# Batches 0 and 1 of a fused attention and ELU-FFN kernel: weights in blocks of 1024 columns, eight shared PSUM banks and a given order of TensorE's first groups; halves of M merged in every batch

## The chip, the cores and the metric

The kernel runs on one core of a Trainium2 chip. The core has a matrix engine (TensorE, PE in the profile, with its weight loads as PEld), a vector engine (VectorE, DVE), a scalar engine (ScalarE, ACT), GpSimd (POOL), a queue engine (SyncE, SP) that issues most DMAs, and 16 DMA engines. Each engine runs its own instructions in the order in which they were emitted and waits for others through semaphores. TensorE writes only to PSUM, eight banks of 128 rows by 512 float32 values. The metric is the device time of one execution in microseconds (us).

## The reference

There are 8 batches of 8 heads with 512 tokens and 32 states of width 64. Each token attends to the states and each state to the tokens; the joined result (544 rows a batch, 512 wide) goes through a feed-forward layer with an ELU.

```python
def _attn_ref(x, state):
    scores = scale * np.matmul(x, state.transpose(0, 1, 3, 2))
    ...
    xread = np.matmul(a, state)           # a = softmax(scores)
    scores2 = scale * np.matmul(state, x.transpose(0, 1, 3, 2))
    ...
    sread = np.matmul(a2, x)              # a2 = softmax(scores2)
    return np.concatenate([xread, sread], axis=2).astype(np.float32)

def _moe_ref(x, w_in, w_out):             # x: (4352, 512)
    h = x @ w_in                          # w_in: 512 x 2048, float64
    g = np.where(h > 0.0, h, alpha * (np.exp(np.minimum(h, 0.0)) - 1.0))
    return (g @ w_out).astype(np.float32) # w_out: 2048 x 512, float64
```

The weights come as float64, 8 MB each, so that every weight has to be turned into float32 on the chip.

## The kernel before

**A planner orders everything.** The kernel first lists all operations in program order (`Plan.add`, each with an estimated cost and the tiles it reads and writes), then `Plan.run` plays them through once: each engine takes, of its ready operations, TensorE the one with the lowest number and every other engine the one that is due first (`set_due` works the due times back from TensorE's own order). The result is one fixed order for each engine, emitted at the end (lines 1366 to 1371). All operations are therefore recorded by one line of the kernel, L413; the fills of line 1361 are the exception. PSUM banks are given out in program order to the operations that open them, from six free banks; banks 6 and 7 are kept for one accumulator of the later batches (line 505). In the first 40 us of the plan, TensorE's idle time is filled with matmuls of the identity into bank 7 (`fill`).

**Weights.** `weight_block` (line 1015) loads a block of 64-bit words (128 rows, 512 values) by DMA into one of six raw buffers; `convert` (line 988) makes float32 of it with two ScalarE and four VectorE operations (`tensor_scalar` twice, `scalar_tensor_tensor`, and an unsigned add). There are 32 blocks: 16 of w_in, two for each of the eight column blocks `hc` of 256, and 16 of w_out. The float32 columns of w_in are kept in DRAM (`w_in_mem`) and fetched again for each later batch (`fetch`, into one of three slots, `hc % 3`).

**One batch.** Token attention is folded into the first layer: M = states times w_in (`make_m`, one half of a 512-wide chunk at a time, 16 small matmuls in a 64-row by 32-column tiling of the array), and h = a times M. `scores` (line 600) makes the scores, `softmax` (line 666) both softmaxes (VectorE, ScalarE, and GpSimd for two products), `state_read` reads for the states. In batches 0 and 1, `ffn1_plain` forms h with 512-wide matmuls, four groups for each of four chunks; from batch 2 on, `ffn1_chunk` and `ffn2` use Strassen-Winograd forms (seven products for eight), the second layer in two levels. Their sums of operands run on VectorE and GpSimd.

**The order of the program.** `start()` (line 1041) does batches 0 and 1 up to the middle of the second layer: a step `w_step(hc)` for each column block (convert, `make_m` for both batches, copy), with the attention and `ffn1` between them, then w_out's conversion and the second layer. Then `ffn2(o, 1, x1)` ends batch 1, `batch(b)` does batches 2 to 7, and `states()` the state rows of all batches. Each `ffn2` (line 1154) makes the scores, softmax and first half of M of the next batch in passing: `make_m` 0 and 1 stand ahead of the steps of `second[7]` (lines 1197 and 1199), `make_m` 2 and 3 ahead of those of `second[5]` (lines 1213 and 1214), 4 to 7 in `batch` (lines 1266 to 1275). `ident_ready` (line 1030) clears the two kept banks with four identity matmuls each.

## Time and profile before

| | |
|---|---|
| median of 3 runs | 726.34 us (725.87 to 726.53) |
| the profiled execution's own time | 725.68 us |
| its span, first to last instruction | 723.9 us |
| PE, PEld busy | 712.2, 594.0 us (98, 82%) |
| DVE, ACT, POOL busy | 544.9, 292.4, 131.3 us (75, 40, 18%) |
| TensorE clock granted | full, in all 40 slices |
| fills (L1361) | 148 matmuls |

A busy share is a union of instructions' times; TensorE's instructions overlap in its pipeline, so that its 98% also covers fills and short waits. A timeline line gives start, length, engine, line, operation, tiles (out<-in), shape and count; in brackets stand the idle time before it and what ended it. A matmul of float32 appears as two MATMUL instructions.

### The profile page before, as it was taken

To read this page: it belongs to the slowest core of one execution; us is meant where nothing else is said; L and a number is where in the kernel's file an instruction comes from. 1 tells how busy PE (TensorE), PEld (TensorE's weight loads), DVE (VectorE), ACT (ScalarE), POOL (GpSimd) and SP (SyncE) were. 2 spreads that over 40 slices of the span, in tenths; PEclk is the share of its full clock that TensorE was granted. 3 is DMA by queue.
4 is the path that set the end of the run, shared out by engine and by line. 5 is a ranking of instruction groups with operands and counts; after the bars stand their busy time and mean duration, and the time that the engine had idled before them with its cause. 6 is when DMAs were issued, how large, how long until landed. Compare 5 with 4: busy or idle time off the path is not lost.

```text
span 723.9 us, 14101 instructions
## 1 busy us (share of the span) xinstructions
PE 712.2 (98%) x5588; PEld 594.0 (82%) x5588; DVE 544.9 (75%) x1030; ACT 292.4 (40%) x576; POOL 131.3 (18%) x158
## 2 busy tenths in 40 slices
PE   9999999999999999999999999999999999999998
PEld 8744468888988798878988898879887898899886
DVE  2999999999658984898678975898489866976230
ACT  3899983011056213732074315621273207410320
POOL 0210000033111251108020521125110803000000
PEclk9999999999999999999999999999999999999999
DMA  9859970022262334425172326343442423000500
GB/s 231 265 123 320 293 254 29 1 52 96 88 146 82 100 84 120 114 59 138 70 172 61 81 67 150 103 104 84 117 117 59 125 81 118 1 1 30 152 27 25
DMA packets 133250, 78.52 MB, mean 108 GB/s; under 512 B 114240, under 2 KB 114752, under 8 KB 133184
## 3 DMA queue, kind: packets, MB, share of 16 engines
q1 hardware_dynamic: 130744, 76.96, 38.2%
q10 hardware_dynamic: 2440, 0.66, 0.5%
q8 instruction: 44, 0.72, 0.4%
q14 instruction: 22, 0.18, 0.1%
HBM read 61.34 MB, written 13.11 MB: 103 GB/s over the span
## 4 chain that ended last, share of the span: by engine, by line
PE 61%; DVE 29%; issue 3%; ACT 3%; POOL 2%; DMA 1%; SPq 1%; DVEq 0%; POOLq 0%; ACTq 0%
PE ps L413 60%; DVE g L413 7%; DVE sec L413 4%; DVE s L413 4%; DVE small L413 3%; DVE t_w L413 1%; POOL soft L413 1%; DVE w_out L413 1%; DVE ps L413 1%; DVE soft L413 1%; DVE o L413 1%; ACT xe L413 1%; DVE xr L413 1%; DVE m L413 1%; PE ps L1361 1%
## 5 line engine op out<-in xcount | busy, mean ns | idle before, releaser
L413 PE MATMUL ps<-w_out,g 128*128 128x256 f32 (+1 forms) x960 | 174.3, 332 | 0.5
L413 PEld LDWEIGHTS ps<-w_out,g 128*128 128x128 f32 x960 | 150.5, 191 | 21.1 <-ACT o L413 4.2
L413 PE MATMUL ps<-aT,m 128*128 128x256 f32 (+1 forms) x568 | 148.4, 407 | 1.2 <-ACT read L413 0.7
L413 PEld LDWEIGHTS ps<-aT,m 128*128 128x128 f32 x568 | 105.7, 190 | 32.6 <-issue 16.6
L413 DVE TENSOR_TENSOR o<-o,ps 128x128 f32<-128x128 f32 (+2 forms) x214 | 59.9, 286 | 60.2 <-PE ps L413 58.5
L413 POOL TENSOR_TENSOR m<-m 128x256 f32<-128x256 f32 x72 | 57.0, 810 | 192.4 <-ACT m L413 191.0
L413 ACT ACTIVATE xe<-ps 128x512 f32<-128x512 f32 x104 | 60.6, 599 | 59.2 <-PE ps L413 43.2
L413 PE MATMUL ps<-sec 128*128 128x128 f32 x544 | 73.5, 278 | 3.5 <-DVE o L413 3.5
L413 PEld LDWEIGHTS ps<-sec 128*128 128x128 f32 x544 | 66.2, 192 | 9.2 <-DVE o L413 7.1
L413 PE MATMUL ps<-t_w,s 128*128 128x128 f32 (+1 forms) x448 | 68.8, 305 | 0.0
L413 DVE SCALAR_TENSOR_TENSOR g<-xe,ps 128x512 f32<-128x512 f32 x56 | 37.1, 682 | 40.3 <-ACT xe L413 36.1
L413 PEld LDWEIGHTS ps<-t_w,s 128*128 128x128 f32 x448 | 62.6, 191 | 4.8 <-ACT m L413 0.8
L413 POOL TENSOR_TENSOR soft<-soft,small 128x512 f32<-128x512 f32 x32 | 35.1, 1101 | 153.4 <-DVE small L413 152.9
L413 ACT COPY o<-ps 128x128 f32<-128x128 f32 (+2 forms) x55 | 21.8, 408 | 85.3 <-PE ps L413 82.2
L413 ACT COPY ps<-ps 128x512 f32<-128x512 f32 x24 | 13.7, 570 | 95.8 <-PE ps L413 95.8
L413 ACT COPY m<-ps 128x512 f32<-128x512 f32 (+1 forms) x56 | 26.8, 530 | 57.5 <-PE ps L413 57.5
L413 PE MATMUL ps<-aT,s 128*128 128x256 f32 x168 | 41.5, 382 | 0.0
L413 DVE TENSOR_SCALAR xe<-xe 128x512 f32<-128x512 f32 x48 | 20.4, 431 | 27.7 <-ACT xe L413 27.5
L413 POOL TENSOR_TENSOR s<-s 128x256 f32<-128x256 f32 x24 | 17.0, 727 | 133.7 <-ACT s L413 133.2
L413 PE MATMUL ps<-w_half,kT 64*32 64x256 f32 x1024 | 39.8, 385 | 0.7 <-DVE g L413 0.4
L413 DVE TENSOR_TENSOR ps<-sec,ps 128x512 f32<-128x512 f32 x48 | 32.6, 690 | 8.3 <-PE ps L413 4.9
L413 ACT COPY sec<-ps 128x512 f32<-128x512 f32 x48 | 28.0, 584 | 22.4 <-PE ps L413 22.2
(112 smaller groups left out, 1074.4 us busy)
## 6 DMA issues: line engine op xcount, KB each, us to landing
w_half<-w_in_mem SPq DMA_DIRECT2D x56, 512.0 KB
t_w<-in_moe_w_in_dram SPq DMA_DIRECT2D x16, 512.0 KB
t_w<-in_moe_w_out_dram SPq DMA_DIRECT2D x16, 512.0 KB
out_dram<-o SPq DMA_DIRECT2D x14, 512.0 KB
xe<-in_x_dram SPq DMA_DIRECT2D x26, 256.0 KB
o<-in_x_dram SPq DMA_DIRECT2D x80, 64.0 KB
w_in_mem<-w_half SPq DMA_DIRECT2D x8, 512.0 KB
xr<-xr SPq DMA_DIRECT2D x96, 32.0 KB
```

The source lines that it names most:

```text
L413: ins = getattr(engine, name)(**{k: resolve(v) for k, v in kw.items()})
L1361: nc.tensor.matmul(psum[:, 7, :P], ident, ident, start=False, stop=True, skip_group_check=True)
```

## The change

Seven things change. **Weights** come in blocks of 1024 values (three raw buffers, 16 blocks); only the first block of w_in is loaded and converted in two parts. **The first loads** have a given order (`FIRST_LOADS`), and the states of batch 0 and of batch 1 are turned apart. **The program's order** in `start()`: `ffn1` of batch 0, chunk 0, stands ahead of `turn_state` and of batch 1's attention, and `ffn1` of batch 1 ahead of `turn_state(1)`; `FIRST_PE` gives 70 of TensorE's operations in `start()` other places in its order (an operation's `turn`), among them the first products of the second layer, and `EARLIER` shifts the due times of some 70 operations. **PSUM**: all eight banks are shared until the kept ones are first used, and an operation takes a free bank whenever it can run, not in program order. `ident_ready` now depends on the last TensorE operation of `start()`; fills go to any bank that the plan has free, from 0.5 us of idle time on and one in 0.3 us. **The planner's estimates** are others: 0.115 us between dependent VectorE operations, 0.1 us when TensorE changes its tiling, other DMA rates. **Halves of M**: `make_m` takes both halves in one operation from batch 2 on; the first pair (`first_m`) stands behind `scores`, the second ahead of `state_read`. **Softmax**: five small VectorE operations fewer for each batch, where the two groups' scalars are now handled together. The state softmax lies in `sec_2` (batches 0 and 1) or in `xr`, and `read` in `kT`.

The diff, cut to its core:

```diff
-    FREE_BANKS = 6
+    BANKS = 8
...
-        DVE: {PE: 0.15, DVE: 0.0, ACT: 0.12, POOL: 0.16, SP: 0.2},
+        DVE: {PE: 0.15, DVE: 0.115, ACT: 0.12, POOL: 0.16, SP: 0.2},
...
-        POOL: {PE: 0.12, DVE: 0.08, ACT: 0.08, POOL: 0.0, SP: 0.2},
+        POOL: {PE: 0.12, DVE: 0.08, ACT: 0.08, POOL: 0.1, SP: 0.2},
...
+    TURN = 0.1
+    KEPT_BANKS = 0
...
+            op.turn = self.places.get(op.number, op.number)
...
+        self.kept = {b.first: b.fixed for b in self.fixed}
+        self.all_banks = min([op.number for op in self.kept], default=0)
...
+        for op in sorted((op for op in self.ops if op.engine == PE), key=lambda op: op.turn):
+            op.due = at
+            at += op.cost
...
-                took = op.cost + self.LANDING + op.moved / 250e3
+                took = op.cost + self.LANDING + op.moved / op.rate
...
+            op.due -= op.nudge
+        for op in self.ops:
+            if op.rank is not None:
+                op.due = op.rank - 1e6
...
+        def choice(op):
+            if op.number < self.all_banks:
+                return banks
+            return [b for b in banks if b[1] not in fixed]
+
+        def pick(e):
+
...
+                later = [coming[e][0][0]] if coming[e] else []
+                for _, n, op in able[e]:
+                    start = max(at, ready[op])
+                    if op.port:
+                        start = max(start, port)
+                    if op in self.opening or op in self.kept:
+                        t = bank_time(op)
+                        if t is None:
+                            continue
+                        start = max(start, t)
+                    if op.moved and len(lanes) >= 8:
+                        start = max(start, lanes[-8] + 0.1)
+                    if start <= at + 1e-9:
+                        return at, op
+                    later.append(start)
...
+            if e == PE and op.shape != shape:
+                at += self.TURN
+                shape = op.shape
...
+    def make_m(b, *hcs):
+        c = hcs[0] // 2
+        if hcs[0] % 2 == 0:
             st[b, "m", c] = [bank(), bank()]
-        by_state(
-            b, st[b, "m", c], [w[:, m] for m in range(NP)], slice(h * 256, (h + 1) * 256), 0.52,
-            start=h == 0, name="make_m",
-        )
+        calls = []
+        for hc in hcs:
+            w, h = st["w", hc], hc % 2
+            calls += by_state(
+                b, st[b, "m", c], [w[:, m] for m in range(NP)],
+                slice(h * 256, (h + 1) * 256), h == 0,
+            )
+        products(0.46 * len(hcs), calls, "make_m", "state")
...
+    def soft_a(b, g):
+        return (sec_2 if b < 2 else xr[:, 1024:])[:, g * 512 : (g + 1) * 512]
+
+    def read(b):
+        return kT[:, B + b if b < 2 else b - 1]
...
         for g in range(G):
             V.transpose(out=soft_t(g), in_=s[g])
             V.reduce_max(out=tops(g)["top"], in_=s[g], axis=AX_X)
-            V.tensor_scalar(
-                out=tops(g)["top"], in0=tops(g)["top"], scalar1=-scale, scalar2=None, op0=ALU.mult
-            )
+        V.tensor_scalar(out=top, in0=top, scalar1=-scale, scalar2=None, op0=ALU.mult)
...
+            V.reduce_sum(out=tops(g)["total_t"], in_=rows(g), axis=AX_X)
+        V.tensor_scalar(out=total_t, in0=total_t, scalar1=eps, scalar2=None, op0=ALU.add)
+        V.reciprocal(out=total_t, in_=total_t)
         for g in range(G):
-            total_t = tops(g)["total_t"]
-            V.reduce_sum(out=total_t, in_=rows(g), axis=AX_X)
-            V.tensor_scalar(out=total_t, in0=total_t, scalar1=eps, scalar2=None, op0=ALU.add)
-            V.reciprocal(out=total_t, in_=total_t)
-            Q.tensor_tensor(out=rows(g), in0=rows(g), in1=bc(total_t, NS), op=ALU.mult)
+            Q.tensor_tensor(
+                out=rows(g), in0=rows(g), in1=bc(tops(g)["total_t"], NS), op=ALU.mult
+            )
             V.transpose(out=to[:, g * 512 : (g + 1) * 512], in_=soft_t(g))
-            total = tops(g)["total"]
-            V.tensor_scalar(out=total, in0=total, scalar1=eps, scalar2=None, op0=ALU.add)
-            V.reciprocal(out=total, in_=total)
+        V.tensor_scalar(out=total, in0=total, scalar1=eps, scalar2=None, op0=ALU.add)
+        V.reciprocal(out=total, in_=total)
...
-        q = raw[:, 0].rearrange("p (n k) -> p n k", n=2)
+        n = raw.shape[1]
+        q = raw[:, : n // 2].rearrange("p n (j k) -> p (n j) k", j=2)
...
     raws = [
-        t_w_sb.rearrange("p i k q -> p (i k q)")[:, i * 1024 : (i + 1) * 1024].bitcast(U32)
-        .rearrange("p (n k) -> p n k", n=2)
-        for i in range(6)
+        t_w_sb[:, i].rearrange("p k q -> p (k q)").bitcast(U32).rearrange("p (n k) -> p n k", n=4)
+        for i in range(3)
     ]
...
+    def weight_block(n, parts=1):
+
+        out = []
+        for i in range(parts):
+            k = 4 // parts
+            rows = slice(i * k, (i + 1) * k)
+            raw = raws[n % 3][:, rows]
+            if n < 8:
+                src, dst = w_in_v[:, rows, n * 512 : (n + 1) * 512], w_half[:, n % 3, rows]
+            else:
+                q, c = divmod(n - 8, 4)
+                rows = slice(4 * c + i * k, 4 * c + (i + 1) * k)
+                src = w_out_v[:, rows, q * 512 : (q + 1) * 512]
+                dst = w_out[:, rows, q * 256 : (q + 1) * 256]
+            dma(raw, src, kind="load_w")
+            out.append((dst, raw))
+        return out
...
     def ident_ready(i):
         v = fixed[i].view()
+        late = [op for op in plan.ops if op.engine == PE][-1]
...
+        plan.ops[-1].deps.add(late)
+
+    FIRST_PE = (
+        153, 48, 171, 198, 258, 106, 104, 86, 327, 32, 165, 16, 190, 265, 214, 157, 331, 90, 232,
+        410, 335, 277, 261, 248, 169, 45, 289, 161, 202, 35, 146, 149, 347, 186, 210, 102, 339,
+        173, 183, 408, 94, 229, 269, 218, 319, 194, 206, 98, 281, 113, 411, 293, 304, 414, 109,
...
+    )
+    FIRST_LOADS = (
+        6, 9, 0, 3, 5, 4, 1, 8, 7, 2, 12, 10, 11, 13, 14, 15,
+    )
+    EARLIER = {
+        23: 34, 43: -2, 74: -5, 85: 22, 96: -17, 100: -12, 119: 28, 124: 25, 132: -3, 134: 2,
...
+    }
...
-        load_states(0, 2, raw_s, (SP, ACT))
-        load_x(0, x_halves, (SP, ACT))
         blocks = {}
 
         def read_block(n):
             blocks[n] = weight_block(n)
 
-        for n in range(6):
-            read_block(n)
-            if n == 3:
-                load_x(1, x_1)
-        turn_states(raw_s, 0, 2)
+        def convert_block(n):
+            for dst, raw in blocks[n]:
+                convert(dst, raw)
+            if n + 3 < 16:
+                read_block(n + 3)
+
+        n = len(plan.ops)
+        load_states(0, 1, raw_s, (SP, ACT))
+        blocks[0] = weight_block(0, 2)
+        load_x(0, x_halves, (SP, ACT))
+        load_states(1, 2, raw_s[:, 1:], (SP,))
+        read_block(1)
+        load_x(1, x_1)
+        read_block(2)
+        first = plan.ops[n:]
+        for k, i in enumerate(FIRST_LOADS):
+            first[i].rank = k
+        turn_states(raw_s[:, 0:1], kT[:, 0:1])
...
         def w_step(hc):
-            for r in range(2):
-                n = 2 * hc + r
-                convert(*blocks[n])
-                read_block(n + 6)
-            w = w_half[:, hc % 3]
+            convert_block(hc)
+            w = st["w", hc] = w_half[:, hc % 3]
             c = hc // 2
-            make_m(0, hc, w)
+            make_m(0, hc)
             copy_m_half(0, hc, m_sb[:, c % 2])
-            make_m(1, hc, w)
+            if hc == 0:
+                turn_states(raw_s[:, 1:2], kT[:, 1:2])
+            make_m(1, hc)
             dma(w_in_mem[:, hc], w, tokens=((), (f"mem{hc}",)), kind="keep_w")
             if c < 3:
                 copy_m_half(1, hc, m1[c])
             elif hc == 7:
                 copy_m(1, 3, m1[3])
 
-        def ffn1(c):
-            ffn1_plain(0, c, g0, a_sb, e_slots)
-            ffn1_plain(1, c, g_sb, aT1, e_slots)
+        def ffn1(b, c):
...
         w_step(0)
         turn_x(x_halves, ob)
         scores(0, ob)
         softmax(0, a_sb)
         w_step(1)
-        turn_state()
-        state_read(0)
+        ffn1(0, 0)
+        turn_state(0)
         turn_x(x_1, ob)
         scores(1, ob)
+        state_read(0)
         softmax(1, aT1)
-        turn_state()
+        w_step(2)
+        ffn1(1, 0)
+        turn_state(1)
         state_read(1, x_1)
-        ffn1(0)
-        w_step(2)
         w_step(3)
-        ffn1(1)
+        ffn1(0, 1)
+        ffn1(1, 1)
         w_step(4)
         load_states(2, B, raw_t, (SP,))
-        turn_states(raw_t, 2, B)
+        turn_states(raw_t, kT[:, 2:B])
         w_step(5)
-        ffn1(2)
+        ffn1(0, 2)
+        ffn1(1, 2)
         w_step(6)
         w_step(7)
-        ffn1(3)
-        for n in range(16, 32):
-            convert(*blocks[n])
-            if n + 6 < 32:
-                read_block(n + 6)
+        ffn1(0, 3)
+        ffn1(1, 3)
+        for n in range(8, 16):
+            convert_block(n)
...
+    def first_m(b):
+        fetch(0)
+        fetch(1)
+        make_m(b, 0, 1)
+        copy_m(b, 0, m_to[0])
+        sum_m(m_to[0])
+        fetch(2)
+        fetch(3)
...
             if nxt:
                 scores(b + 1, xr)
-                fetch(0)
-                fetch(1)
+                first_m(b + 1)
...
             sum_a()
-        if nxt:
-            make_m(b + 1, 0, st["w", 0])
-            fetch(2)
-            make_m(b + 1, 1, st["w", 1])
-            copy_m(b + 1, 0, m_to[0])
-            sum_m(m_to[0])
-            fetch(3)
-        else:
+        if not nxt:
             turn_read()
+        elif not six:
+            first_m(b + 1)
...
-        if nxt:
-            make_m(b + 1, 2, st["w", 2])
-            make_m(b + 1, 3, st["w", 3])
-            copy_m(b + 1, 1, m_to[1])
-            sum_m(m_to[1])
...
         steps = second[4].steps(c21)
         second[3].sums(o.a12, s_2[0])
         if nxt:
+            make_m(b + 1, 2, 3)
+            copy_m(b + 1, 1, m_to[1])
+            sum_m(m_to[1])
             state_read(b + 1)
...
-        make_m(b, 4, st["w", 4])
+        make_m(b, 4, 5)
         fetch(7)
-        make_m(b, 5, st["w", 5])
         copy_m(b, 2, m_to[2])
...
-        make_m(b, 6, st["w", 6])
-        make_m(b, 7, st["w", 7])
+        make_m(b, 6, 7)
...
     o, x1 = start()
+    plan.places = dict(zip(FIRST_PE, sorted(FIRST_PE)))
+    for n, t in EARLIER.items():
+        plan.ops[n].nudge = t
     ident_ready(0)
     ident_ready(1)
     ffn2(o, 1, x1)
...
-    def fill():
+    def fill(i):
         tc.keep_in_program_order(
             nc.tensor.matmul(
-                psum[:, 7, :P], ident, ident, start=False, stop=True, skip_group_check=True
+                psum[:, i, :P], ident, ident, start=True, stop=True, skip_group_check=True
             )
         )
 
-    steps, fills = plan.order(3, fill, 40.0)
```

## The prediction

> **What bounds the kernel now.** I read the page first, then TensorE's timeline of the start, the busy times of the stages, VectorE's timeline, and TensorE's timeline of one later batch.
>
> ```profile
> span 723.9 us, 14101 instructions
> PE 712.2 (98%) x5588; PEld 594.0 (82%) x5588; DVE 544.9 (75%) x1030; ACT 292.4 (40%) x576; POOL 131.3 (18%) x158
> PE 61%; DVE 29%; issue 3%; ACT 3%; POOL 2%; DMA 1%; SPq 1%; DVEq 0%; POOLq 0%; ACTq 0%
> ```
>
> TensorE's 98% hides two things. 148 of its matmuls are fills, and VectorE holds 29% of the chain of waits. TensorE's timeline of the start:
>
> ```profile
> 17.56 1.60 PE L413 MATMUL ps<-w_half,kT 64*32 64x256 f32 x32
> 19.09 3.17 PE L1361 MATMUL ps<-ident 128*128 128x128 f32 x26
> ...
> 31.85 1.60 PE L1361 MATMUL ps<-ident 128*128 128x128 f32 x12
> 34.16 1.99 PE L413 MATMUL ps<-aT,m 128*128 128x512 f32 x4 [0.71 <-ACT read L413]
> ```
>
> Matmuls whose source is `ident` alone are fill. The first group of the first layer begins at 34.16 us; the other groups before it (turnings, scores twice, M four times, one read) add up to some 10 us. So some 23 us of the start are idle for TensorE. Busy times by stage (PE, PEld, DVE, ACT, POOL):
>
> ```profile
> 13.00:40.00 27.00, 26.21 (x384) 18.77 (x383) 23.75 (x58) 22.97 (x52) 7.55 (x8) 1.00 0.76 223
> 40.00:101.50 61.50, 60.83 (x324) 26.57 (x323) 60.53 (x115) 58.15 (x118) 0.79 (x1) 1.00 0.83 256
> 101.50:145.00 43.50, 42.70 (x209) 36.39 (x207) 41.69 (x61) 12.35 (x22) 0.00 (x0) 1.00 0.17 58
> ```
>
> From 40 to 145 us VectorE is 96 to 98% busy and ScalarE 95% until 101.5; TensorE is about full too. An earlier start helps only if VectorE is relieved as much. What VectorE does first (its timeline):
>
> ```profile
> 13.69 0.89 DVE L413 TENSOR_SCALAR w_half<-w_half 128x512 f32<-128x512 f32 x2 [2.67 <-ACT w_half L413]
> 14.49 0.68 DVE L413 SCALAR_TENSOR_TENSOR t_w<-t_w 128x512 uint32<-128x512 uint32 x1
> 15.21 0.69 DVE L413 CUSTOM_DVE_ANT_0 w_half<-w_half,t_w 128x1024 uint16<-128x1024 uint16 x1
> 15.82 0.88 DVE L413 TENSOR_SCALAR w_half<-w_half 128x512 f32<-128x512 f32 x2
> ```
>
> One block takes it 15.82 - 13.69 = 2.13 us. Four of them and the first softmax, whose last transpose ends at 30.99 us, stand ahead of the first layer. In a later batch (the second layer, next to the M of batch 3):
>
> ```profile
> 245.79 1.09 PE L413 MATMUL ps<-w_half,kT 64*32 64x256 f32 x32
> 247.31 1.16 PE L413 MATMUL ps<-sec 128*128 128x128 f32 x8 [0.42 <-DVE o L413]
> ...
> 254.29 0.66 PE L413 MATMUL ps<-w_half,kT 64*32 64x256 f32 x16
> ...
> 258.65 0.66 PE L413 MATMUL ps<-w_half,kT 64*32 64x256 f32 x16
> ```
>
> Here TensorE waits for VectorE once for 0.42 us and, from the same timeline, at 249.63 for 0.27 us. A half of M alone holds TensorE from 254.29 to 254.88, 0.59 us; two together 1.02 us (296.58 to 297.60). The period from one batch to the next, between equal places of the chain of waits (302.91 to 381.46), is 78.55 us.
>
> **The change, part by part.**
>
> (a) *The start, to the first group.* The first weight block is now fourth on SP's queue and in two parts. Before, SP issued it at 5.41 us, after x and the states; three issues of 0.5 to 0.8 us put it now at about 2.7 us. ScalarE converted first at 12.96 us, behind two copies of turned x of 1.07 us. 2.7 + 1.0 us earlier puts VectorE's first work at about 10.0 instead of 13.69. It then has two old-size blocks (4.3 us), one new one (3.7, below), and the softmax: ten wide operations at 0.6 to 0.66 us plus small ones, 7.5 us. 10.0 + 4.3 + 3.7 + 7.5 = 25.5, and 0.7 for waits on GpSimd: 26.2 us. The attention of batch 1, which before stood in TensorE's order between 24.64 and 31.85, now stands behind this group and no longer delays it; nor does the bank that the read held (0.71). Start 34.16 to 26.2: **-8.0 us**. Bounds: -3.2 if only the way from 30.99 to 34.16 goes, -10.2 if the group starts as soon as scores (16.25) and an undisturbed softmax of 8 us allow it.
>
> [...] four GpSimd products lie in the softmax. [...] The rows: these GpSimd products take 1.05 us, at most 1.34; beside them stood shorter operations, though. The nearest row is the worst of them, 4 x 0.29 = 1.2 us; I take the 0.7 above [...].
>
> (b) *Conversions.* For 1024 values no row of this kind stands in the trace. A `tensor_tensor` of 1024 follows another after 1.26 us when it depends on it (313.40 to 314.66), 1.13 when not; the two `tensor_scalar` gain about 0.25 us each for 512 more values (0.42 us against 0.17 for 16 values). Sum: 0.80 + 0.50 + 1.26 + 1.13 = 3.7 us for what took 4.26. Fifteen times: 8.6 us of VectorE, 6.3 of it before 101.5. Three softmaxes lose five small operations of 0.1 to 0.35 us each, some 0.9 us a batch. ScalarE: copies of 256 and 512 take 0.37 and 0.59 us, so 0.15 us of fixed time for each of 30 operations, 4.5 us. On TensorE's path these are worth nothing by themselves; they are the cover for (a). VectorE has 3.7 (start) + 6.3 + 1.8 = 11.8 us of lead at 101.5, against 8.0 that TensorE gains, so TensorE stays the bound. Without the cover (a) would be eaten by 145 us.
>
> (c) *The first layer, 34.16 to 101.54 us.* 128 matmuls at 0.429 us are 54.9, with M, reads and turnings 62.9; it took 67.4, so 4.5 us are lost to switches and waits. Eight banks for six, the choice of any group that can run, and first products of the second layer as fillers: I take **-1.3**, bounds -3 and +1.
>
> (d) *`ident_ready`.* Before, its 16 matmuls ran at 1.36 us, when nothing else could. Now they wait for the end of `start()`, where TensorE is the bound: 16 x 0.112 = 1.8 us. Less 0.3 for VectorE's lead there: **+1.5**, bounds +0.5 and +1.8.
>
> (e) *Later batches.* Two pairs of halves stood apart in each: 2 x 0.59 - 1.02 = 0.16, and about 0.09 for the slow first matmul after each visit: 0.25 a pair, **0.5** a batch. The waits for VectorE (0.69 with the two above) fall in a stretch in which VectorE works without a pause; there the softmax is 0.9 us shorter, but the halves 2 and 3 (1.18 us of TensorE's work) leave it for a place behind it, so that TensorE comes to its later operands sooner. Net -0.3; what waits then is `second[5]` and `second[4]`, for VectorE's sums. Of DMAs, `fetch(7)` goes out behind both halves instead of one, 0.4 us later, among 16 block loads on SP's queue; in the trace it is issued at 282.81 and its M comes at 296.58, so nothing. `fetch(5)` and `fetch(6)` go out some 5 us later and still have about 15. -0.8 a batch, five whole periods: **-4.0**; one pair in the last batch: **-0.25**. Bounds for all: -8 and +4.
>
> (f) *Fewer fills.* [...] The row shows full clock in all 40 slices under dense fills; [...]. [...] by the row nothing, which I take.
>
> Sum: -8.0 - 1.3 + 1.5 - 4.0 - 0.25 = -12.05, so a span of 711.9. The profiled execution took 725.68 us, 1.8 more than its span: 713.7. The median of the runs is 0.66 above the profiled one: **714.3 us**.
>
> **The rivals.**
>
> *The start gains little* (chance 0.22). Priority lists order only what is ready; if block 1, now one DMA of 1 MB behind x, comes late, the first group starts at 31. For it: ScalarE and VectorE are both near full from 30 us on. Against: the idle VectorE before 13.69. -3.2 + 0 + 1.8 - 4.25 = -5.7: 720.6 us.
>
> *All terms at their good bounds* (0.16): -10.2 - 3 + 0.5 - 8 = -20.7: 705.6 us. For it: the planner now counts 0.115 us between dependent VectorE operations, which the trace shows (1.26 against 1.13), so its order may avoid most waits.
>
> *Slower* (0.07): the stretch of the second layer that has lost its cover. If VectorE's order there makes TensorE wait more than 12.05/6 = 2.0 us more in each of six batches, all is gone; at 3 us the time is 714.3 + 18 - 0.3 = 732. For it: VectorE is without a pause from 228.7 to 258. Against: the wait now is 0.7, and only 1.18 us of cover go.
>
> *The change does nothing that can be measured* (0.03): start and later batches cancel.
>
> **How the numbers follow.** My forecast, with 709 to 718 around it, has 0.52; with the others that makes 1. A measurement of this kernel tells about 0.2% (1.5 us) from no change. Faster: 0.52 + 0.22 + 0.16 = 0.90; same 0.03; slower 0.07. The range of 8 in 10 leaves out the slow case, most of no change and the end of the good one: 705 to 721.5.
>
> **What would show it.** Right: the first 128x512 group near 26 us, TensorE's second layer (first 128x256 group) near 92, a period of about 77.7 us, M always in 32s from batch 2 on, 16 identity matmuls in the middle. Wrong: VectorE idle before 13 us as before; waits of TensorE for VectorE above 1 us in each batch; a clock below full in the first slices.

## The result, and the profile after

The changed kernel takes **717.43 us** (median of 4 runs, 715.9 to 719.57) against 726.38 (4 runs, 725.87 to 726.53). The ratio is 0.988, interval 0.9854 to 0.9907. The profiled execution took 717.05 us with a span of 715.3. The forecast was 714.3 us, its range 705 to 721.5. The time lies in the range, but its parts do not lie where the forecast put them; that the total fits is in part luck.

The page of the changed kernel, its head, the engines' busy time and the chain that ended last:

```profile
span 715.3 us, 13801 instructions
PE 700.3 (98%) x5526; PEld 588.3 (82%) x5526; DVE 525.5 (73%) x931; ACT 285.3 (40%) x547; POOL 122.7 (17%) x158
PE 73%; DVE 14%; ACT 7%; DMA 4%; issue 1%; SPq 0%; DVEq 0%
```

VectorE's share of the chain fell from 29% to 14%. ScalarE's rose from 3 to 7% and DMA's from 1 to 4%: something new holds the chain. To find where, four marks that have the same work behind them in both kernels serve: the first 128x512 group, the scores of batch 2, the scores of batch 3 and those of batch 7.

| stretch | before | after | difference | forecast |
|---|---|---|---|---|
| start to the first 128x512 group | 34.16 | 28.63 | -5.53 | -8.0 |
| from there to the scores of batch 2 (first layer and more) | 109.98 | 115.65 | **+5.67** | -1.3 |
| scores of batch 2 to scores of batch 3 (holds the identity products) | 91.74 | 92.64 | +0.90 | +1.5 - 0.8 = +0.7 |
| scores of batch 3 to scores of batch 7 (four periods) | 313.94 | 307.27 | **-6.67** | -3.2 |
| scores of batch 7 to the end | 174.04 | 171.07 | -2.97 | -0.25 |
| span | 723.86 | 715.26 | -8.60 | -12.05 |

The scores of batch 2 stand at the same place in both kernels, first in the one before, then in the changed one (TensorE's timelines):

```profile
144.14 1.09 PE L413 MATMUL ps<-soft,kT 64*32 64x512 f32 x16
```

```profile
144.28 1.09 PE L438 MATMUL ps<-xr,kT 64*32 64x512 f32 x16
```

So all that the start gains is lost again before the scores of batch 2, and what remains comes from the batches, which gain twice the forecast. TensorE's timeline of the changed kernel (start, duration, form, count, idle time before it and its releaser):

```profile
24.22 2.00 PE L438 MATMUL ps<-o,kT 64*32 64x512 f32 x16
25.93 1.15 PE L438 MATMUL ps<-w_half,kT 64*32 64x256 f32 x16
27.01 1.10 PE L438 MATMUL ps<-xe,xr 128*32 128x64 f32 x64
28.04 0.66 PE L438 MATMUL ps<-w_half,kT 64*32 64x256 f32 x16
28.63 5.42 PE L438 MATMUL ps<-aT,m 128*128 128x512 f32 x12
...
51.12 1.98 PE L438 MATMUL ps<-s,g 128*128 128x512 f32 x4 [1.87 <-DVE g L438]
...
78.20 1.13 PE L438 MATMUL ps<-w_out,sec 128*128 128x256 f32 x4 [1.25 <-DVE w_out L438]
...
113.00 2.21 PE L438 MATMUL ps<-w_out,sec 128*128 128x256 f32 x9 [1.21 <-DVE w_out L438]
```

From its first 128x512 group to the scores of batch 2 TensorE waits 6.0 us in all; in the kernel before it was 1.5. At 51.12 it has waited 1.87 us for VectorE. VectorE itself had been waiting for ScalarE, and ScalarE for a weight block, as ScalarE's and VectorE's timelines show:

```profile
42.81 0.53 ACT L438 COPY kT<-ps 128x384 f32<-128x384 f32 x1
47.11 1.13 ACT L438 ACTIVATE t_w<-t_w 128x1024 f32<-128x1024 uint32 x1 [3.78 <-DMA t_w<-in_moe_w_in_dram]
```

```profile
46.24 0.67 DVE L438 TENSOR_SCALAR w_half<-w_half 128x1024 f32<-128x1024 f32 x1
49.78 0.69 DVE L438 TENSOR_SCALAR w_half<-w_half 128x1024 f32<-128x1024 f32 x1 [2.87 <-ACT w_half L438]
```

The block that ScalarE waits for was issued at 40.87 and landed at 47.09 us. The next was issued at 50.02 and landed at 56.17, and ScalarE waits for it again (1.21 us at 56.19), as it does later for blocks of w_out (1.91 us at 74.65, 1.94 at 101.66). In the kernel before it waits for no block between 28 and 145 us.

Counted from 0, these are blocks 5 and 6. Each needs the buffer of a block three places earlier. VectorE's last operations on those ended at 37.48 and 46.31 us, 3.4 and 3.7 us before the two issues. What SP did meanwhile stands in its timeline:

```profile
38.81 1.94 SPq L438 DMA_DIRECT2D xe<-in_x_dram  x2
40.87 0.56 SPq L438 DMA_DIRECT2D t_w<-in_moe_w_in_dram  x1
...
42.03 7.89 SPq L438 DMA_DIRECT2D xe<-in_x_dram  x7
50.02 0.57 SPq L438 DMA_DIRECT2D t_w<-in_moe_w_in_dram  x1
```

It issued loads of x, which stand ahead of the weight loads in its order. So a block is late by its buffer and by its place in SP's queue. The same three stages as before:

```profile
13.00:40.00 27.00, 23.17 (x293) 12.55 (x292) 24.50 (x46) 24.21 (x49) 9.11 (x8) 0.94 0.86 236
40.00:101.50 61.50, 58.16 (x358) 26.83 (x351) 54.42 (x71) 50.87 (x89) 0.00 (x0) 1.00 0.81 263
101.50:145.00 43.50, 41.98 (x195) 33.65 (x193) 37.80 (x43) 13.73 (x20) 0.00 (x0) 1.00 0.14 42
```

From 40 to 101.5 us VectorE was 98% busy before and is 88% busy now (54.42 of 61.50); TensorE went from 60.83 to 58.16. VectorE has time to spare now, but TensorE gets no more done. And in a later batch (TensorE's timeline, scores and M of the next batch in one run):

```profile
313.81 1.09 PE L438 MATMUL ps<-xr,kT 64*32 64x512 f32 x16
314.69 1.07 PE L438 MATMUL ps<-w_half,kT 64*32 64x256 f32 x32
...
324.91 1.16 PE L438 MATMUL ps<-sec 128*128 128x128 f32 x8 [0.26 <-DVE o L438]
```

The period is 76.80 us (313.81 to 390.61) instead of 78.55, and the waits for VectorE's `o` in it are 0.26 us instead of the 0.71 in the same period before:

```profile
325.64 1.16 PE L413 MATMUL ps<-sec 128*128 128x128 f32 x8 [0.44 <-DVE o L413]
327.96 1.16 PE L413 MATMUL ps<-sec 128*128 128x128 f32 x8 [0.27 <-DVE o L413]
```

### The profile page after: what moved, and what is told of

Its sections match the earlier page's. It is cut to its first block, busy times and chain, and to the rows that moved or that the text cites. A ratio compares the mean times of both kernels' runs of the same rounds, so it can differ in the third digit from the quotient of the medians.

```text
span 715.3 us, 13801 instructions
## 1 busy us (share of the span) xinstructions
PE 700.3 (98%) x5526; PEld 588.3 (82%) x5526; DVE 525.5 (73%) x931; ACT 285.3 (40%) x547; POOL 122.7 (17%) x158
## 4 chain that ended last, share of the span: by engine, by line
PE 73%; DVE 14%; ACT 7%; DMA 4%; issue 1%; SPq 0%; DVEq 0%
PE ps L438 73%; DVE g L438 3%; DVE small L438 2%; DMA t_w<-in_moe_w_in_dram 2%; ACT sec L438 2%; DVE sec L438 2%; ACT xe L438 2%; DVE s L438 1%; DVE w_out L438 1%; DMA t_w<-in_moe_w_out_dram 1%; DVE xr L438 1%; DVE soft L438 1%; ACT w_half L438 1%; ACT t_w L438 1%; DVE t_w L438 1%
## 5 line engine op out<-in xcount | busy, mean ns | idle before, releaser
L438 ACT ACTIVATE xe<-ps 128x512 f32<-128x512 f32 x104 | 58.9, 599 | 60.4 <-PE ps L438 47.8
L438 POOL TENSOR_TENSOR m<-m 128x256 f32<-128x256 f32 x72 | 51.5, 735 | 164.1 <-ACT m L438 162.7
L438 PE MATMUL ps<-t_w,s 128*128 128x128 f32 (+1 forms) x448 | 70.3, 306 | 0.0
L438 PE MATMUL ps<-w_half,kT 64*32 64x256 f32 x1024 | 36.5, 385 | 0.2 <-DVE w_half L438 0.2
L438 PEld LDWEIGHTS ps<-aT,s 128*128 128x128 f32 x168 | 31.9, 190 | 4.3
L438 ACT ACTIVATE xe<-xe 128x512 f32<-128x512 f32 x56 | 33.4, 634 | 0.6
```

Of the source, the lines that this page charges most:

```text
L438: ins = getattr(engine, name)(**{k: resolve(v) for k, v in kw.items()})
```

## The experiments

Three disputes. **Supply or order**: is the start's gain lost because each 1 MB load waits for a whole conversion, three buffers being all there are, or because the given order of TensorE's groups suits the chip badly? **Merging or planner**: what shortens the batch? **Clock**: does the sparser fill cost time? The marks of each profile (us; the period is the median of the four from the scores of batch 3 to those of batch 7):

| run | time (median) | first 128x512 | scores, batch 2 | batch 2 to 3 | period |
|---|---|---|---|---|---|
| before | 726.38 | 34.16 | 144.14 | 91.74 | 78.5 |
| after | 717.43 | 28.63 | 144.28 | 92.64 | 76.8 |
| blocks 3 to 5 in `w_out` | 711.22 | 27.39 | 137.84 | 92.83 | 76.8 |
| weights hardly loaded | 711.94 | 27.88 | 138.77 | 92.83 | 76.8 |
| halves of M apart | 722.76 | 28.09 | 144.51 | 94.21 | 77.68 |
| before, with halves merged | 728.85 | 35.49 | 144.35 | 91.55 | 79.1 |
| old estimates | 723.83 | 29.88 | 140.38 | 93.62 | 78.13 |
| without the two lists | 719.92 | 31.02 | 146.84 | 92.83 | 76.7 |
| six banks, without the lists | 720.87 | 32.08 | 151.34 | 91.05 | 76.8 |
| early identity products, dense fills | 720.32 | 38.99 | 149.39 | 91.34 | 76.7 |
| one old estimate (VectorE) | 729.08 | 27.94 | 144.95 | 93.43 | 78.47 |
| `w_out`, without the lists | 714.77 | 31.11 | 142.00 | 92.83 | 76.6 |
| `w_out`, cheap identity products | **709.34** | 29.00 | 138.69 | 91.49 | 76.6 |
| the same, with the old fills | 710.87 | 28.96 | 138.61 | 91.48 | 76.8 |

**Blocks 3 to 5 in the empty part of `w_out`.** The edit changes the place where three loads land and nothing else:

```diff
-            raw = raws[n % 3][:, rows]
+            raw = (
+                raws[n % 3] if n not in (3, 4, 5)
+                else w_out[:, 24 - 4 * n : 28 - 4 * n].bitcast(U32)
+            )[:, rows]
```

> The changed kernel, but weight blocks 3, 4 and 5 land in the part of w_out that nothing fills yet, so that their loads need not wait until an older block is converted. Work and order lists are as in the changed kernel. Supply theory (the start gains 5.5 us and loses it again by the third attention because each load of 1 MB waits for a whole conversion and lands 6 to 9 us later): scores of batch 2 at 139 to 141 us instead of 144.28, time 712 to 714 us. Rival, order theory (the fixed order of TensorE's first groups fits the chip badly, whenever the weights come): scores of batch 2 stay within 1 us of 144.3, time 717 us.

711.22 us (710.52 to 711.66), ratio to before 0.9789, interval 0.9775 to 0.9804. Scores of batch 2 at 137.84, 6.4 us earlier than in the changed kernel and beyond the expectation of 139 to 141; 1.2 us of these are there at the first group already. SP issues the three loads between 17.1 and 18.9 us, ahead of those loads of x. Block 5 lands at 31.44 instead of 47.09 us, block 6 at 35.41 instead of 56.17. The stages:

```profile
13.00:40.00 27.00, 23.37 (x353) 13.39 (x352) 24.53 (x45) 25.57 (x54) 9.12 (x8) 1.00 1.03 346
40.00:101.50 61.50, 60.52 (x309) 27.95 (x309) 60.08 (x79) 54.98 (x91) 0.00 (x0) 1.00 0.76 231
101.50:145.00 43.50, 43.50 (x213) 37.32 (x212) 37.68 (x45) 10.68 (x20) 2.06 (x2) 1.00 0.06 19
```

The DMA engines are full in the first stage (346 GB/s against 236), VectorE is 98% busy again in the second, and TensorE has no gap in the third. TensorE's waits up to the scores of batch 2 fall from 6.0 to 2.2 us. The supply theory holds with the size of nearly the whole loss: late blocks cost it. Whether the buffers or the loads of x ahead in the queue made them late isn't separated, since the early loads pass both. The order of SP's queue alone was not tested.

**Weights hardly loaded.** The same question without another place for the data:

```diff
-            dma(raw, src, kind="load_w")
+            if n > 2:
+                dma(raw[:, :, :8], src[:, :, :8], kind="load_w")
+            else:
+                dma(raw, src, kind="load_w")
```

> The changed kernel, but of every weight block from the fourth on only a sliver (8 of 512 columns of each row) is loaded; the rest is whatever the buffer holds, so the weights are wrong, and the output too. All conversions, products and copies stay. Supply theory: an upper bound of what it can give back, scores of batch 2 at 138 to 140 us, time 711 to 713 us. Order theory, or VectorE's own work as the bound: scores of batch 2 at 143 to 144.5 us, time 716 to 717.5 us.

711.94 us; scores of batch 2 at 138.77, 5.5 us earlier. With almost no weight traffic the start is no better than with full traffic from free buffers, so the DMA engines can carry the whole traffic in time. But the chance to issue is no better here: block 5 is issued at 41.14 us, as late as in the changed kernel, and block 6 at 46.64, 3.4 us earlier than there. They land at 44.04 and 49.14, 3 and 7 us earlier. ScalarE still waits 2.66 us for block 5, and yet the loss is gone. So a late issue costs that much only together with the 6 us that a full block takes to land.

**Without the two lists** (the order theory's own test, on both supplies):

```diff
-    plan.places = dict(zip(FIRST_PE, sorted(FIRST_PE)))
-    for n, t in EARLIER.items():
-        plan.ops[n].nudge = t
```

> The changed kernel without the fixed order of TensorE's first groups and without the earlier due times (the order of the first loads stays): the planner orders the start by the program's own order. Supply theory: the weights set the pace up to the third attention whatever the order, scores of batch 2 at 143.5 to 146 us, time 717 to 719 us. Order theory (the lists fit the chip badly): scores of batch 2 at 142 us or less, time 715 us or less. If the lists are worth what an earlier first group suggests: scores of batch 2 at 148 us or more.

719.92 us, scores of batch 2 at 146.84, first group at 31.02. That is 2.6 us later than with the lists, somewhat beyond the 146 that supply alone allowed and less than the 148 of lists that keep all of the earlier start. The order theory falls: without the lists it gets worse, not better. Nearly all of the 2.6 us, 2.4, is there at the first group already.

> The version with weight blocks 3 to 5 landing in w_out, without the fixed order of TensorE's first groups and without the earlier due times. Under three buffers the lists were worth 2.6 us at the scores of batch 2 (144.28 against 146.84). If they only save what the late weights cost: scores of batch 2 within 0.7 us of 137.84 and 711 us. If they order the first softmax and conversions well in themselves: 2 us or more later, 713 us or more. If they were made for late weights and hinder early ones: earlier than 137 us, 710 us or less.

714.77 us, scores of batch 2 at 142.00 against 137.84 with the lists. With early weights the lists are worth 4.2 us, more than under late ones: they order the start well in itself. Again most of it, 3.7 us, is there at the first group (31.11 against 27.39). Some 1 us of that can be the clock: from 26 to 28 us it was 0.62 on the mean in this profile and full in the other; what it costs is worked out in (f) below.

**Six banks from the beginning** (on the version without the lists):

```diff
-        self.all_banks = min([op.number for op in self.kept], default=0)
+        self.all_banks = 0
...
-        plan.ops[-1].deps.add(late)
+        plan.places[plan.ops[-1].number] = i - 10
```

> As the run without the two lists, and besides with six shared banks from the start on, two kept apart, and their identity products first of all as in the kernel before. Set against the run without the lists. By the forecast the late identity products cost 1.5 to 1.8 us behind the third attention, which comes back: from scores of batch 2 to scores of batch 3 91.0 us instead of 92.6. If eight banks are worth something in the first layer, scores of batch 2 come 1 to 3 us later than there; if not, within 0.5 us.

720.87 us (719.81 to 723.92). The identity products give back 1.78 us between the scores of batches 2 and 3 (92.83 to 91.05; expected 91.0). The time is 0.95 us longer all the same, so by the medians eight banks are worth 0.95 + 1.78 = 2.7 us ahead of the scores of batch 2. The profile says 4.5 (151.34 - 146.84), but it was the slowest of the four. Its mean clock was also lower, 0.991 over the profile against 0.998 in that of the run without the lists. How much of the 2.7 us is the clock, and whether six banks bring the lower clock about, stays open.

**Halves of M apart again**, at their old places:

```diff
-        make_m(b, 4, 5)
-        fetch(7)
+        make_m(b, 4)
+        fetch(7)
+        make_m(b, 5)
...
-            make_m(b + 1, 2, 3)
-            copy_m(b + 1, 1, m_to[1])
-            sum_m(m_to[1])
             state_read(b + 1)
```

> The changed kernel with the halves of M apart again and at the places they had before, in every batch from the third on (and the third batch's own first halves). Start and first layer as in the changed kernel. If merging and its new places are what shortens a batch: period back near 78.4 us instead of 76.8, time 726 us. If the planner's new estimates and its freedom among eight banks give most of it, and merging only the forecast 0.5 us a batch: period 77.3 us, time about 720 us.

722.76 us, period 77.68, between the two expectations (78.4 and 77.3). Merging is worth 0.88 us a batch here, 1.57 between batches 2 and 3. TensorE has no wait for VectorE in the period from 316.41 to 394.09 us: the new planner with the halves apart is 0.8 us a batch faster than the kernel before.

**The kernel before with merging alone**:

```diff
-        make_m(b, 4, st["w", 4])
-        fetch(7)
-        make_m(b, 5, st["w", 5])
+        make_m(b, 4, 5)
+        fetch(7)
...
-                fetch(0)
-                fetch(1)
+                first_m(b + 1)
```

> The kernel before with one edit: the halves of M are computed in pairs and at the new places (the first pair right behind the scores, the second ahead of the read). If merging gives the gain of a batch: period 76.9 us instead of 78.5, time 718 us. If it gives only the forecast 0.5 us a batch and the planner the rest: period 78.0 us, time 723.5 us. If the old planner can't use it (six banks given out in a fixed order, M holding two of them for longer): period 78.5 us or more, time 726 us or more.

728.85 us, ratio 1.0029, interval 1.0017 to 1.0041: **slower**, period 79.1. TensorE's timeline of one batch shows why:

```profile
327.81 1.16 PE L413 MATMUL ps<-sec 128*128 128x128 f32 x8 [1.00 <-DVE o L413]
329.14 1.16 PE L413 MATMUL ps<-t_w,m 128*128 128x128 f32 x8 [0.17 <-DVE o L413]
...
341.66 1.16 PE L413 MATMUL ps<-t_w,s 128*128 128x128 f32 x8 [0.64 <-DVE o L413]
```

1.81 us of waits for VectorE in place of 0.71. The halves of M that stood between TensorE's operations in the second layer were its cover. These waits grew by 1.1 us and the period by 0.6.

**The planner's old estimates** in the changed kernel:

```diff
-        DVE: {PE: 0.15, DVE: 0.115, ACT: 0.12, POOL: 0.16, SP: 0.2},
+        DVE: {PE: 0.15, DVE: 0.0, ACT: 0.12, POOL: 0.16, SP: 0.2},
...
-        POOL: {PE: 0.12, DVE: 0.08, ACT: 0.08, POOL: 0.1, SP: 0.2},
+        POOL: {PE: 0.12, DVE: 0.08, ACT: 0.08, POOL: 0.0, SP: 0.2},
...
-    TURN = 0.1
+    TURN = 0.0
```

> The changed kernel with the planner's three old estimates: nothing between dependent VectorE or dependent GpSimd operations, nothing for a change of the matmul's shape. Which groups may run, and the eight banks, stay. With the halves apart the period was 77.68 us against 78.54 of the kernel before, so 0.86 us of a batch come from the planner. If the estimates give it: period 77.5 us or more, time 722 us or more. If the free choice among groups and banks gives it: period 76.8 us, time within 1.5 us of 717.4.

723.83 us (20 runs, 720.94 to 727.36), period 78.13: 1.33 us a batch. The free choice of groups and banks alone doesn't give the gain. TensorE waits 0.60 and 0.55 us for VectorE in one batch.

**The VectorE estimate alone** back to 0:

```diff
-        DVE: {PE: 0.15, DVE: 0.115, ACT: 0.12, POOL: 0.16, SP: 0.2},
+        DVE: {PE: 0.15, DVE: 0.0, ACT: 0.12, POOL: 0.16, SP: 0.2},
```

> The changed kernel with one estimate back at its old value: nothing between dependent VectorE operations instead of 0.115 us. The three estimates together made the period 78.13 us instead of 76.80. If the VectorE one is what counts: period 77.9 to 78.2 us, time 722 to 725 us. If it is the time for a change of the matmul's shape: period 76.8 to 77.1 us, time 717 to 719 us.

729.08 us, period 78.47: 1.67 us a batch from this one number, more than from the three together. Two of its waits, from TensorE's timeline of one batch:

```profile
329.18 1.16 PE L438 MATMUL ps<-sec 128*128 128x128 f32 x8 [0.59 <-DVE o L438]
...
389.10 1.10 PE L438 MATMUL ps<-aT,m 128*128 128x256 f32 x4 [0.56 <-DVE ps L438]
```

They make 1.15 us where the changed kernel has 0.26. The old estimates together gave the same two waits, so these come with VectorE's estimate. They are 0.9 of the 1.67 us; the rest wasn't taken apart. Against the old estimates together its profiled span is 5.9 us longer (725.1 and 719.2), and 4.6 of these stand before the scores of batch 2 (144.95 against 140.38): each estimate schedules the start anew too. How an estimate moves the start can't be read from one profile, though; that of the old estimates is the fastest of its 20 runs.

**Early identity products and dense fills**, on the version with blocks in `w_out`. This version alters what the two kept banks hold when the first halves accumulate there, so it is read for its times alone:

```diff
-                while at < until and t + 0.5 < at:
+                while at < until and t + 0.3 < at:
...
-                    t += 0.3
+                    t += 0.13
...
-                (v[:, k * P : (k + 1) * P], ident, ident, dict(start=k == 0, stop=True))
-                for k in range(4)
+                (v[:, :8], ident, ident[:, :8], dict(start=True, stop=True))
...
+    for i in (6, 7):
+        for k in range(4):
+            tc.keep_in_program_order(
+                nc.tensor.matmul(
+                    psum[:, i, k * P : (k + 1) * P], ident, ident, start=k == 0, stop=True,
+                    skip_group_check=True,
+                )
+            )
```

> The version with weight blocks 3 to 5 landing in w_out, and two mends more: the identity products of the two kept banks run first of all, in the time in which TensorE waits for x, and only 8 columns of each are done again behind the start; fills stand 0.13 us apart in the plan instead of 0.3. The first should give 1.6 us back between scores of batch 2 and of batch 3 (92.83 to 91.2 us). The second: if the half clock of the changed kernel's first 30 us matters, the first group comes earlier than 27.39 us and scores of batch 2 earlier than 137.84; if the fills stand in the way, later by up to 1 us. Time 709 to 710 us; rival, nothing of it shows: 711 us.

The first half came as expected (92.83 to 91.34 us). The second didn't: it cost 11.6 us of the start (137.84 to 149.39) where I allowed "up to 1 us". TensorE's timeline of the start:

```profile
1.36 3.78 PE L1437 MATMUL ps<-ident 128*128 128x128 f32 x16 [1.36 <-POOL ident masks.py:199]
4.93 9.86 PE L1428 MATMUL ps<-ident 128*128 128x128 f32 x86
14.72 0.28 PE L438 MATMUL ps<-ident,g 64*128 64x64 f32 x2
```

The turning of the first state begins at 14.72 us instead of 8.00: 86 MATMUL instructions of fills and 16 of the identity products stand in TensorE's order ahead of it, at 0.115 to 0.24 us each. 720.32 us.

**Cheap identity products**, late as in the changed kernel, on the version with blocks in `w_out`:

```diff
-                (v[:, k * P : (k + 1) * P], ident, ident, dict(start=k == 0, stop=True))
-                for k in range(4)
+                (v[:, k * 256 : (k + 1) * 256], half[:, :P], half, dict(start=k == 0, stop=True))
+                for k in range(2)
```

with `half = ident.bitcast(mybir.dt.bfloat16)`.

> The version with weight blocks 3 to 5 landing in w_out, with the late identity products made in two bfloat16 pieces of 256 columns for each bank instead of four float32 pieces of 128 (what they leave there is overwritten before it is used). Two banks took 1.78 us; this should take 0.8 us, all of it on TensorE's path: scores of batch 2 to scores of batch 3 91.8 us instead of 92.83, time 710.2 us. If something else ends last there (VectorE), the time stays at 711.2 us.

709.34 us (709.16 to 709.78), ratio to before 0.9765, interval 0.975 to 0.978: the fastest of all, 8.1 us below the changed kernel. Both banks take 0.60 us in one run:

```profile
160.53 0.60 PE L438 MATMUL ps<-ident 128*128 128x256 bf16 x4
```

The stretch fell by 1.34 us, more than the 1.0 expected.

**The old rule for fills** on top of that:

```diff
-                while at < until and t + 0.5 < at:
+                while at < until and t + 0.3 < at:
...
-                    t += 0.3
+                    t += 0.25
```

> The version with blocks 3 to 5 landing in w_out and the cheap late identity products, with the rule for fills of the kernel before (an idle stretch above 0.3 us in the plan gets one fill for each 0.25 us, instead of above 0.5 and each 0.3). Without it the profile showed half the clock from 23.5 to 27 us, the first group of the first layer at 29.00 us and the scores of batch 2 at 138.69, against 27.39 and 137.84 in the run that kept its clock. If the half clock costs time once the weights no longer set the pace: first group at 27.5 us, scores of batch 2 at 137.9, time 708.5 us. If VectorE's work behind it takes the difference up anyway, or the fills stand in the way: 709.3 us or more.

710.87 us (710.1 to 713.27), no gain, rather 1.5 us more. Yet the clock stayed up: its mean is 1.0 in all five runs with the old fills, 0.997 or 0.998 in the four with the sparse ones. The windows (the third number from the right is the granted clock), first with the sparse fills, then with the old ones:

```profile
24.00:26.00 2.00, 2.00 (x20) 0.94 (x27) 1.40 (x4) 2.00 (x4) 1.67 (x1) 0.50 1.05 401
26.00:28.00 2.00, 2.00 (x68) 0.84 (x56) 1.63 (x3) 1.68 (x4) 1.24 (x2) 0.72 1.07 375
```

```profile
24.00:26.00 2.00, 2.00 (x39) 1.14 (x37) 1.48 (x4) 2.00 (x4) 1.60 (x1) 1.00 1.07 397
26.00:28.00 2.00, 1.91 (x94) 1.11 (x79) 1.55 (x3) 2.00 (x5) 1.32 (x2) 1.00 1.03 381
```

The first group starts at 29.00 in the one and 28.96 us in the other. That does not show that the lapse is free: at full clock TensorE comes to its read 1 us sooner (26.40 instead of 27.38 us), and then loses it to a half of M that takes 1.2 us and to a fill at 28.64, just ahead of the group. (f) has a cleaner pair.

## Why the prediction was right and wrong

The total came out inside the range because two errors have opposite signs: 9.4 us too much hoped for the start and the first layer, 6.2 us too little for the batches after the scores of batch 3. That they nearly cancel is luck. (One sum of the forecast was off as well: 16.25 and 8 us put the good bound of (a) at -9.9, not -10.2.)

**(a) The start: direction right, size off by 2.5 us.** VectorE's first conversion starts at 9.46 us (forecast 10.0), so the way to it was right. What was missing is seen in its timeline:

```profile
9.46 0.89 DVE L438 TENSOR_SCALAR w_half<-w_half 128x512 f32<-128x512 f32 x2 [0.93 <-ACT w_half L438]
...
13.48 0.69 DVE L438 SCALAR_TENSOR_TENSOR t_w<-t_w 128x512 uint32<-128x512 uint32 x1 [1.55 <-ACT w_half L438]
...
25.82 0.71 DVE L438 STREAM_TRANSPOSE aT<-soft 128x512 f32<-128x512 f32 x1 [0.87 <-POOL soft L438]
26.63 0.72 DVE L438 STREAM_TRANSPOSE soft<-ps 128x512 f32<-128x512 f32 x1
27.27 0.67 DVE L438 STREAM_TRANSPOSE aT<-soft 128x512 f32<-128x512 f32 x1
```

The forecast let the first group follow the softmax's last transpose at 26.2 us; that transpose ends at 27.94. Two things not in its sum make up most of the 1.7 us: VectorE idles 1.55 us for ScalarE's part of the second half block, and a transpose of batch 1's scores (0.72) stands in between. ScalarE had copied turned x until 12.06 and then waited 0.15 us for that half block, which landed at 12.19:

```profile
12.22 0.67 ACT L438 ACTIVATE t_w<-t_w 128x512 f32<-128x512 uint32 x1 [0.15 <-DMA t_w<-in_moe_w_in_dram]
```

But the last transpose is not what the group waits for. In the run with the halves of M apart, with the same order of TensorE here, the group starts at 28.09 us, before that transpose ends (28.39). It needs the first one, which ends at 26.53 in the changed kernel, and then stands behind TensorE's own work, which has no gap from 23.33 us on: the scores of batch 1 at 24.22, a half of M, the read, another half. The forecast had said that batch 1's attention "now stands behind this group and no longer delays it". That step was wrong: its scores still stand ahead, without the lists too (28.34, group at 31.02). The clock made this work about 1 us longer, see (f).

The waits on GpSimd came out near the estimate. Of four GpSimd products in this softmax three took 1.05 us and one 1.91 us, from 23.88 to 25.78; beside it ran VectorE's add of a conversion, 1.22 us from 23.66. VectorE then waited the 0.87 us shown above for it. Taken: 0.7; measured: 0.87. Whether the add made the product longer was not tested.

**(b) Conversions: right, and beside the point.** One block of 1024 columns takes VectorE 0.60 + 0.60 + 1.14 + 1.13 = 3.5 us between starts (forecast 3.7). VectorE is less busy as forecast. But the step from VectorE's lead of 11.8 us to "so TensorE stays the bound" counted only VectorE's work. It left out what its work waits for. That is the step that failed: **the cover was there, but a block has to arrive before it can be converted.** With blocks of 1 MB and three buffers a load waits for the whole conversion of an older block, then for the loads of x ahead of it on SP's queue (3.4 and 3.7 us for blocks 5 and 6), and then takes 6 us to land; in the kernel before, a load waited for the conversion of half as much. The rival "the start gains little" named a late block, but looked for it at block 1 and at the first group. It was blocks 5 and 6, and two of w_out after them, and the price was paid in the first layer, where the forecast put -1.3 and its worst bound was +1.

**(c) The first layer: wrong, by the step above.** With the supply freed the stretch takes 137.84 - 27.39 = 110.45 us, against 109.98 before. So even then the stretch gains nothing: it is 0.5 us longer. The long run of the second layer begins at 105.87 us in the changed kernel and at 101.48 with the supply freed; it was 101.54 before, and the forecast had put its beginning near 92. VectorE is full there again (98% busy from 40 to 101.5 us), but that it alone explains the +0.5 wasn't tested. The lists do little for this stretch: without them it takes 0.2 us more under late weights (115.82 against 115.65) and 0.4 under early ones. What they are worth lies ahead of the first group. Eight banks may give up to 2.7 us, with the clock's part in it unknown.

**(d) The identity products: right.** Moving them to the beginning gave 1.78 us back between the scores of batches 2 and 3, and the rows below, 0.89 us each up to the next group, say the same; the 0.3 us of lead that I deducted was not there.

```profile
166.12 1.05 PE L438 MATMUL ps<-ident 128*128 128x128 f32 x8
...
176.03 1.06 PE L438 MATMUL ps<-ident 128*128 128x128 f32 x8
```

**(e) The batches: right in direction, half the size.** Taken was -0.8 a batch, -0.5 of it merging and -0.3 the waits. Measured is -1.67 a period. A batch's work is 75.5 us of TensorE in every kernel here (176 matmuls at 0.216, 280 at 0.112, scores, M and read 6.1); what lies above it was 3.0 before and is 1.3 now. Undoing merging gives back 0.88, undoing the estimate of 0.115 us between dependent VectorE operations 1.67; the new planner without merging gains 0.8, and merging under the old planner costs 0.6. **The parts don't add up, they need each other**: merging takes a cover away from TensorE (its waits rise from 0.71 to 1.81 us under the old planner), and with the order that counts VectorE's own latency they are 0.26. The waits are the part that the traces show; they are not the whole gain. The forecast had the evidence, 1.26 against 1.13 us between dependent and other operations in the trace, but spent it on a rival of 0.16. In the last stretch (-2.97 against -0.25) two pairs of M lie behind the scores of batch 7, not one, and a wait of 0.52 us at 622.90 is gone; the rest of that difference wasn't taken apart.

**(f) The clock: the lapse came, and its price shows at the first group but not later.** The profile of the changed kernel grants half the clock from 23.55 to 26.96 us, 3.4 us long:

```profile
22.00:24.00 2.00, 1.80 (x21) 1.43 (x21) 2.00 (x7) 2.00 (x6) 0.12 (x1) 0.89 1.07 335
24.00:26.00 2.00, 2.00 (x23) 0.60 (x28) 1.13 (x3) 2.00 (x4) 2.00 (x2) 0.50 0.91 360
26.00:28.00 2.00, 2.00 (x88) 1.13 (x72) 1.89 (x4) 1.68 (x4) 0.79 (x1) 0.76 0.35 104
```

The row of 40 slices on the page, which the forecast went by, reads 9 throughout here as well: a slice is 18 us long, and 9 stands for 90% or more. TensorE's waits in the microseconds before the lapse are 0.99, 0.34 and 0.21 us:

```profile
20.68 0.66 PE L438 MATMUL ps<-ident,sec 128*128 128x128 f32 x4 [0.99 <-ACT sec L438]
```

What brought the lapse about was not shown.

The run with the halves of M apart has the same order on TensorE here and kept its clock. From the last turnings of batch 1's x to the first group TensorE takes 5.48 us there (22.61 to 28.09) and 6.47 in the changed kernel (22.16 to 28.63). With blocks 3 to 5 in `w_out` it is 5.33 at full clock (22.06 to 27.39) and 6.39 with the lapse (22.61 to 29.00, cheap identity products). So the lapse costs about 1 us at the first group. At the scores of batch 2 nothing of it is left: 144.28 with it and 144.51 without under three buffers; and in three runs in which VectorE's first transpose of the softmax starts alike (26.26, 26.34 and 26.35 us) 138.69 with it, 138.61 without (old fills) and 138.77 without (weights hardly loaded).

Executions of one and the same kernel differ in this too: with the halves of M apart, the same order every time, the mean clock was 1.0 in two of four and 0.998 in the other two. The forecast counted nothing for the clock, which was right for the total, but because VectorE sets the pace behind the first group, as these runs suggest, and not because the clock stayed full.

## What to carry to other kernels

When a relief is counted as cover, follow it back to its source: an engine with spare time is of use only if its data are there in time. Doubling a block while halving the number of buffers postpones each request to the end of a whole block's work, and other loads ahead in the same queue postpone it further. A region of memory that is still empty in that phase can serve as the missing buffers; here another place for three loads gave 6.2 us. A change of order and the planner's latencies belong together: the same merging was worth -0.9 us a batch under the new planner and +0.6 under the old one, and the new planner without its latency for VectorE gave the batch's whole gain back.

## What the runs showed that was not expected

- Blocks of twice the size came no faster. From the trace's events, successive 0.5 MB blocks of the kernel before landed 1.36 and 1.34 us apart (11.61, 12.97, 14.31), successive 1 MB blocks of the version with `w_out` 2.73 and 2.70 us apart (21.91, 24.64, 27.34): about 390 GB/s either way. The longer time from issue to landing, 6 us and more, buys nothing here.
- The kernels differ in how far their times spread: 720.94 to 727.36 us with the old estimates, 726.89 to 733.18 with one of them, 709.16 to 709.78 for the fastest. Late weights alone don't explain it: without the lists, with weights as late, it was 719.14 to 720.57, and with early weights and the old fills 710.1 to 713.27. The cause is open.
- A fill is not free when it is planned too densely: at 0.13 us apart in the plan the fills, 0.115 us for each MATMUL instruction at full clock, delayed the first state's turning by 6.7 us, together with the early identity products.
